# Pooled values of batch 0: four plain slices summed by GpSimd instead of a chain of accumulating transfers

## The chip, the cores and the metric

The kernel runs on one core of one Trainium2 chip. The metric is device time in microseconds (us). Three runs of the kernel before gave a median of 879.14 us (875.92 to 881.02).

## The reference, cut to what matters

Attention over 4 batches, 8 heads, 576 tokens and 64 dimensions per head is followed by two feed-forward layers over the 2304 tokens (512 wide inside 2048). The attention has two parts that are added: a local one over a window of 7 tokens, and a pooled one over averages of 4 tokens, whose result is repeated four times.

```python
q_d = q.reshape(B, H, Sd, factor, D).mean(axis=3)    # factor = 4, Sd = 144
k_d = k.reshape(B, H, Sd, factor, D).mean(axis=3)
v_d = v.reshape(B, H, Sd, factor, D).mean(axis=3)
out_d = sm_attn(q_d, k_d, v_d)
out_up = np.repeat(out_d, factor, axis=2)
...
return (out_up + out_local)
...
h = x @ w_in;  r = np.maximum(h, 0.0);  y = (r * r) @ w_out
...
h = y @ w_in2; out = (h * (1.0 / (1.0 + np.exp(-h)))) @ w_out2
```

The change is about `v_d` of batch 0 only: the sum of four slices of v, each 72 rows by 2 by 512 numbers (288 KB).

## The kernel before, in words

The kernel writes its whole program from generators that a planner (`Schedule`, line 90 on) interleaves. A generator yields the engine it wants next and a cost in us, or an event it waits for, or a lock on one of the PSUM banks; the planner starts whatever can start first by those costs, and ties go to the lower rank. The order in which it lets the generators go on is the order of instructions on each engine's queue; at run time every queue works strictly in that order, and semaphores only make it wait. So a changed cost or a changed event moves instructions of all later stages in the queues.

**The first stage.** Before the first feed-forward matmul the kernel does the attention of the first 512 tokens: `load_qk(0, h)` loads q and k of four head pairs by SyncE (SP), `load_pooled(0)` loads the pooled values, `load_v0` two halves of v, and `eighth("i1", 0)`, `eighth("o1", 0)` the first weights, which arrive as 64-bit numbers and are turned to float32 by ScalarE (line 312) and VectorE (helpers at 268 and 271). For each head pair `pooled(0, hp, SIX)` sums q and k (line 458 or 465), multiplies them (475), takes the softmax (479 to 492), transposes it (498 and 500) and multiplies it with the pooled values (510); ScalarE copies the product out (513). `tile_attention(i, SIX)` does the local attention of 64 tokens at a time, eight of them: scores (586, 589), softmax on VectorE and ScalarE (599 to 617), transposes (626), product with v (638). `tiles_done(0)` (890) adds the two, and gives the event ("xf", 0), on which the first feed-forward matmul (`chunk_in`, line 1027, then 1049) and the second batch's attention hang. All these share six PSUM banks, `pa`, `pb` and `acc0` to `acc3`, through locks. Gaps that the planner sees on TensorE in this stage are filled by `keep_warm` (1540).

**What the steps touch.** `load_pooled(0)` (line 405 on) issues four DMAs from GpSimd's queue (412): the first writes the tile `vd_t`, the three others add to it on the way, and each waits for the one before. `pooled` asks for the bank of its last product before it waits for the event ("pooled", 0). Behind these DMAs on GpSimd's queue stand those of batch 1 (422) and later the sums of batch 1 (432, 434). On SP's queue `load_qk(0)` is followed by one half of v (560), the first weights (304), the other half of v and the second weights. The tile `gr`, which the change uses as a buffer, holds the hidden values of the feed-forward layer from its first chunk on.

Of the kernel before, what the change touches and what calls it, by code (L numbers as in the profile page):

```python
# [13 lines left out]
ALU = mybir.AluOpType  # L14
# [4 lines left out]
NT, DM, DFF = 2304, 512, 2048  # L19
# [11 lines left out]
HG = NG // 2  # L31
# [63 lines left out]
class Schedule:  # L95
# [15 lines left out]
    def mark(self, key):  # L111
        self.events[key] = self.end

    def release(self, name):
        self.locks[name] = self.end
# [59 lines left out]
def tile_attention_two_moes(ctx: ExitStack, tc: tile.TileContext, qw, kw, vw, qt, kt, vt, qp, kp, vp, maskd, tmaskd,  # L175
                            w_in1, w_out1, w_in2, w_out2, out, wide):
    nc = tc.nc
# [5 lines left out]
    V, A, G, PE = nc.vector, nc.scalar, nc.gpsimd, nc.tensor  # L183
# [16 lines left out]
    gr = pool.tile([P, 7 * 512], F32, name="gr")  # L200
# [23 lines left out]
    def words(a, n):  # L224
        return wt[:, a:a + n]
# [40 lines left out]
    def ts(out, in0, s1, op0, s2=None, op1=None):  # L266
        kw_ = {"op1": op1} if op1 is not None else {}
        V.tensor_scalar(out=out, in0=in0, scalar1=s1, scalar2=s2, op0=op0, **kw_)
# [16 lines left out]
    def bank(name, shape):  # L285
        return ps1.tile(shape, F32, tag=name, name=name)
# [105 lines left out]
    def raw_buf(at, n=2048):  # L392
        return words(int(at), n).bitcast(U32)
# [4 lines left out]
    vd_t = dst[0:HG, 4 * NGP + 4 * NG:].rearrange("p (c n) -> p c n", c=2)  # L398
# [6 lines left out]
    def load_pooled(b):  # L405
        yield "DVE", 0.1
        V.memset(qd_t[:, :, NG:], 0.0)
        if b == 0:
            for r in range(4):
                yield "POOL", 1.1  # L410
                yield "DMA", 0.82, 2.0
                G.dma_start(out=vd_t, in_=vp[0, r], **({"accum_op": ALU.add} if r else {}))
        else:
            for r in range(4):
                kw_ = {"accum_op": ALU.add} if r else {}
                if b > 1:
                    yield "POOL", 2.1
                    G.dma_start(out=qd_t[:, :, :NG], in_=qp[b - 2, r], **kw_)
                    G.dma_start(out=kd_t, in_=kp[b - 2, r], **kw_)
                yield "POOL", 1.1  # L420
                yield "DMA", 1.5 if b == 1 else 4.5, 2.0
                G.dma_start(out=vd_t, in_=vp[b, r], **kw_)
        outd[b] = p2.tile([P, 4, NG], F32, tag="outd", name="outd")
        mark(("pooled", b))
# [12 lines left out]
    def pooled(b, hp, banks):  # L437
        pad = PADS[b]
        if b > 1:
            yield "event", ("pooled", b)  # L440
        elif b == 1:
            yield "event", ("sums", b, hp)
        if b == B - 1:
            w = words(hole["o2"] * 1024, 1024)
            yield "event", ("o2", "done")
        elif b == 0 and hp >= 2:
            w = hl[1][:, (hp - 2) * 1024:(hp - 1) * 1024]
        else:
            w = words(EX + (hp % 2) * 1024, 1024)
        n = 1 if b == B - 1 else 2  # L450
        if b:
            yield "event", ("ds", b, hp - n) if hp >= n else ("ds", b - 1, 3 if b > 1 else hp)
        if b == 0:
            yield "event", ("qk", 0, hp)
            for t, src, dve in ((qd_t[:, hp, :NG], qb[:, hp, :], hp in QDVE), (kd_t[:, hp, :], kb[:, hp, 3:3 + S], hp in KDVE)):
                if dve:
                    yield "DVE", 0.67, 0.0
                    V.tensor_reduce(out=t, in_=src.rearrange("p (g r) -> p g r", r=4), axis=AX.X, op=ALU.add)
                    continue
                ba = yield "lock", banks  # L460
                yield "PE", 1.0
                ps = bank(ba, [P, NG])
                src = src.rearrange("p (g r) -> p r g", r=4)
                for r in range(4):
                    PE.matmul(out=ps, lhsT=ident, rhs=src[:, r, :], start=(r == 0), stop=(r == 3))
                yield "ACT", 0.17
                A.activation(out=t, in_=ps, func=AF.Copy)
                release(ba)
        ba = yield "lock", banks
        yield "PE", 0.8, pad  # L470
        ps = bank(ba, [P, 3, NG])
        for c in range(3):
            for j in range(2):
                r = slice(j * D, (j + 1) * D)
                PE.matmul(out=ps[r, c, :], lhsT=qd_t[r, hp, c * QC:c * QC + D], rhs=kd_t[r, hp, :],
                          start=True, stop=True)
        yield "DVE", 0.71, pad
        mx = p2.tile([P, 3], F32, tag="dmx", name="dmx")
        V.tensor_reduce(out=mx, in_=ps, axis=AX.X, op=ALU.max)
        ts(mx, mx, -1.0 / 128.0, ALU.mult)  # L480
        yield "ACT", 1.07, pad
        e = w[:, 0:3 * NG].rearrange("p (c n) -> p c n", c=3)
        pt = w[0:HG, 3 * NG:7 * NG].rearrange("p (k j c q) -> p k j c q", k=2, j=2, c=3)
        sm = p2.tile([P, 3], F32, tag="dsm", name="dsm")
        for c in range(3):
            A.activation(out=e[:, c, :], in_=ps[:, c, :], func=AF.Exp, scale=1.0 / 128.0, bias=mx[:, c:c + 1],
                         accum_out=sm[:, c:c + 1])
        release(ba)
        yield "DVE", 0.93, pad
        ts(sm, sm, 1e-9, ALU.add, 4.0, ALU.mult)  # L490
        V.reciprocal(sm, sm)
        V.tensor_tensor(out=e, in0=e, in1=sm.unsqueeze(2).to_broadcast([P, 3, NG]), op=ALU.mult)
        for kc in range(2):
            ba = yield "lock", banks
            yield "PE", 0.33, pad
            pp = bank(ba, [HG, 3, 2, D])
            for c in range(3):
                PE.transpose(pp[:, c].rearrange("p j q -> p (j q)"), e[:, c, kc * HG:(kc + 1) * HG], ident)
            yield "ACT", 0.29, pad
            A.activation(out=pt[:, kc].rearrange("p j c q -> p c j q"), in_=pp[:, :, :, 0:QC], func=AF.Copy)  # L500
            release(ba)
        ba = yield "lock", banks
        if b < 2:
            yield "event", ("pooled", b)
        yield "PE", 0.6
        po = bank(ba, [P, NG])
        for kc in range(2):
            for j in range(2):
                h = 2 * hp + j
                PE.matmul(out=po[j * D:(j + 1) * D, :], lhsT=vd_t[:, kc, h * D:(h + 1) * D],  # L510
                          rhs=pt[:, kc, j].rearrange("p c q -> p (c q)"), start=(kc == 0), stop=(kc == 1))
        yield "ACT", 0.17
        A.activation(out=outd[b][:, hp, :], in_=po, func=AF.Copy)
        release(ba)
        mark(("ds", b, hp))
# [1031 lines left out]
    with tc.manual_schedule():  # L1547
# [40 lines left out]
        for h in range(4):  # L1588
            add(load_qk(0, h))
        add(load_pooled(0))  # L1590
        convert(0)
        for h in range(2):
            add(load_v0(h))
        for hp in range(4):
            add(pooled(0, hp, SIX))
# [4 lines left out]
        for n in range(1, 16):  # L1600
            convert(n, *([("qk", 0, 3)] if n == 1 else [("at", 3)] if n < 4 else []))
            if n == 3:
                add(split_early(0))
            if n == N1:
                add(load_pooled(1), ("xf", 0))
                for h in range(2):
                    add(load_qk(1, h), ("xf", 0))
                for hp in range(4):
                    add(sums(1, hp), ("xf", 0))
                for hp in range(4):  # L1610
                    add(pooled(1, hp, TWO))
                add(all_pooled(1))
                for i in range(per, 2 * per):
                    add(tile_attention(i, TWO), ("xf", 0))
                add(tiles_done(1))
            if n % 4 == 3 and n >= NFULL:
                add(quarter("i1", n // 4), ("xf", 0))
                add(quarter("o1", n // 4), ("xf", 0))
                add(first_scales(0, 1, n // 4))
# [4 lines left out]
        add(whole("o1"))  # L1624
        add(split_early(1))
        add(load_pooled(2), ("ds", 1), ("at", TPB - 1))
        for hp in range(4):
            add(pooled(2, hp, TWO))
# [14 lines left out]
        r = [[raw_buf(a * 1024)] for a in (22, 26, 28)]  # L1643
# [4 lines left out]
        r = [[gr[:, 1536 + i * 1024:2560 + i * 1024].bitcast(U32) for i in range(2)], [raw_buf(31 * 1024)]]  # L1648
# [122 lines left out]
```

## Time and profile before

| what | us |
|---|---|
| median of three runs | 879.14 |
| lowest and highest run | 875.92, 881.02 |
| span of the profiled execution | 882.3 |
| TensorE busy in it | 851.1 (96%) |
| VectorE busy in it | 673.6 (76%) |
| ScalarE busy in it | 524.6 (59%) |
| GpSimd busy in it | 59.7 (7%) |

The profiled execution is a run of its own; its span, from the first instruction to the last, is the only time that the profile gives for it, and no time around the span is shown. It is 3.2 us longer than the median and 1.3 us longer than the slowest of the three runs. The profile lists, for each engine, when it was busy and what released it after a wait; all times inside it count from the first instruction. TensorE's clock has two levels, 1.2 and 2.4 GHz, and the granted clock is given as a share of the higher one.

### The profile page before, as it was taken

The page shows a single profiled execution, that of the slowest core. Times are in us where ns is not written, and L with a number is a line of the kernel's source. Part 1 is how long each engine was busy: PE and PEld are TensorE (multiplying, and loading weights), DVE is VectorE, ACT ScalarE, POOL GpSimd, SP SyncE. Part 2 cuts the span into 40 slices and gives each one's busy share as a digit, 9 for nine tenths or more (in the row PEclk, how much of TensorE's full clock was granted, in tenths as well). Part 3 has the DMA queues.
Part 4 walks back from the last instruction along what each step waited for, and adds up shares of the span by engine and source line. Part 5 has one row for each costly group of instructions (what it writes and reads, how often), then busy time and mean ns, then how long its engine had stood idle before and what let it go on. Part 6 is the DMA issues. An engine that isn't in the chain of part 4 may idle for free.

```text
span 882.3 us, 14418 instructions
## 1 busy us (share of the span) xinstructions
PE 851.1 (96%) x5578; PEld 507.6 (58%) x5578; DVE 673.6 (76%) x1310; ACT 524.6 (59%) x1026; POOL 59.7 (7%) x86
## 2 busy tenths in 40 slices
PE   8898999999988999999999999999999899999998
PEld 6664554455433444444444445884445778788865
DVE  5567888886667999888988998746988887777731
ACT  3787888888767652435665443666676564344432
POOL 1016113000000400000000000000000110000000
PEclk9899999999999999999999999999999999999999
DMA  9678456844667951242124200322333200010010
GB/s 253 206 200 321 172 157 147 238 164 160 225 201 250 229 135 37 89 155 72 36 84 155 72 28 27 114 61 96 132 113 107 81 25 2 25 49 1 2 48 25
DMA packets 35584, 103.55 MB, mean 117 GB/s; under 512 B 4316, under 2 KB 8540, under 8 KB 32316
## 3 DMA queue, kind: packets, MB, share of 16 engines
q1 hardware_dynamic: 27036, 84.65, 29.0%
q0 software_dynamic: 8192, 17.83, 8.4%
q8 instruction: 44, 0.72, 0.3%
q14 instruction: 24, 0.20, 0.1%
q10 hardware_dynamic: 288, 0.15, 0.1%
HBM read 82.16 MB, written 20.45 MB: 116 GB/s over the span
## 4 chain that ended last, share of the span: by engine, by line
PE 71%; DMA 11%; DVE 8%; ACT 7%; issue 2%; POOL 1%; SPq 0%; POOLq 0%; DVEq 0%; ACTq 0%
PE acc L1106 26%; PE hps L1062 24%; PE seven L1181 6%; PE acc L1216 4%; DMA dst<-vp 4%; DMA wt<-w_in 3%; DMA gr<-w_out 3%; PE hps L1049 2%; DVE ub L1242 1%; DVE gr L271 1%; PE pb L1216 1%; DVE wt L271 1%; ACT sq L333 1%; PE hps L1027 1%; DVE hl L271 1%
## 5 line engine op out<-in xcount | busy, mean ns | idle before, releaser
L1062 PE MATMUL hps<-hl,wt 128*128 128x512 f16 (+1 forms) x1440 | 293.7, 351 | 0.0
L1062 PEld LDWEIGHTS <-wt 128*128 128x128 f16 x1440 | 140.2, 98 | 128.4 <-issue 3.6
L1106 PE MATMUL acc<-gr,wt 128*128 128x512 f16 (+2 forms) x928 | 212.8, 374 | 0.0
L1106 PEld LDWEIGHTS <-wt 128*128 128x128 f16 x864 | 84.5, 99 | 78.3 <-issue 1.2
L271 DVE SCALAR_TENSOR_TENSOR gr<-hps,sc,gr 128x512 f16<-128x512 f32 (+1 forms) x118 | 80.2, 679 | 63.2 <-ACT gr L1476 60.4
L1106 PE MATMUL acc<-wt,gr 128*128 128x512 f16 x480 | 112.0, 379 | 0.1
L1458 ACT ACTIVATE hps<-hps,sc 128x512 f32<-128x512 f32 (+1 forms) x72 | 44.0, 611 | 90.5 <-PE hps L1062 90.2
L1181 PE MATMUL seven<-hl,wt 128*128 128x256 f16 x456 | 80.5, 275 | 5.7 <-DVE ub L1242 5.6
L1473 ACT ACTIVATE hps<-hps,sc 128x512 f32<-128x512 f32 (+1 forms) x46 | 27.4, 596 | 91.5 <-PE hps L1062 87.6
L1106 PEld LDWEIGHTS <-gr 128*128 128x128 f16 x480 | 46.8, 98 | 51.8 <-issue 0.7
L1181 PEld LDWEIGHTS <-wt 128*128 128x128 f16 x672 | 66.1, 98 | 17.9 <-issue 7.5
L1476 ACT ACTIVATE gr<-hps,sc 128x512 f16<-128x512 f32 (+1 forms) x118 | 74.3, 630 | 2.7
L1216 PEld LDWEIGHTS <-gr 128*128 128x128 f16 x672 | 65.6, 98 | 11.0 <-DVE gr L271 2.0
L1216 PE MATMUL acc<-wt,gr 128*128 128x256 f16 x480 | 61.0, 274 | 2.2 <-DVE gr L271 1.1
L1181 PE MATMUL seven<-ub,wt 128*128 128x256 f16 x180 | 49.6, 275 | 0.0
L1242 DVE TENSOR_TENSOR ub<-seven,ub 128x256 f32<-128x256 f32 x74 | 28.6, 419 | 21.8 <-PE seven L1181 20.0
L271 DVE SCALAR_TENSOR_TENSOR wt<-wt,sc 128x1024 f16<-128x1024 f32 x32 | 40.6, 1279 | 4.7 <-ACT wt L372 4.4
L778 DVE TENSOR_REDUCE ub<-ub 128x128 f32<-128x896 f32 x40 | 43.3, 1083 | 1.0
L711 DVE TENSOR_TENSOR ub<-ub,s 128x896 f32<-128x896 f32 x40 | 43.5, 1087 | 0.6
L746 DVE TENSOR_REDUCE s<-ub 128x14 f32<-128x896 f32 x40 | 43.2, 1080 | 0.5
L708 DVE TENSOR_TENSOR ub<-ub 128x896 f32<-128x896 f32 x40 | 43.2, 1081 | 0.0
L271 DVE SCALAR_TENSOR_TENSOR gr<-ub,sc,gr 128x512 f16<-128x512 f32 (+2 forms) x66 | 42.1, 671 | 0.7 <-ACT gr L1476 0.7
(247 smaller groups left out, 1159.1 us busy)
## 6 DMA issues: line engine op xcount, KB each, us to landing
wt<-w_in SPq DMA_DIRECT2D x16, 1024.0 KB, 8.2
wt<-w_out SPq DMA_DIRECT2D x9, 1024.0 KB, 5.5
w<-wt POOLq DMA_DIRECT2D x16, 512.0 KB, 4.6
dst<-w SPq DMA_DIRECT2D x16, 512.0 KB, 3.3
gr<-w_out SPq DMA_DIRECT2D x14, 512.0 KB, 5.4
ub<-vw SPq DMA_DIRECT2D x10, 640.0 KB, 3.8
ub<-kw SPq DMA_DIRECT2D x10, 640.0 KB, 7.2
dst<-vp POOLq DMA_DIRECT2D x16, 288.0 KB, 6.9
```

The source lines that it names most:

```text
L271: V.scalar_tensor_tensor(out=out, in0=in0, scalar=s, in1=in1, op0=op0, op1=op1)
L708: eng.tensor_tensor(out=prod[i % 2].rearrange("p (t w d) -> p t w d", t=2, w=WIN), in0=band(k, j, t0), in1=q[:, j, t0:t0 + 2, :].unsqueeze ...
L711: eng.tensor_tensor(out=prod[i % 2].rearrange("p (t d w) -> p t d w", t=2, d=D), in0=band_v(v, j, t0), in1=prob[u][:, j, t0:t0 + 2, :].uns ...
L746: V.tensor_reduce(out=s[:, j, t0:t0 + 2, :], in_=prod[i % 2].rearrange("p (t w d) -> p t w d", t=2, w=WIN), axis=AX.X, op=ALU.add)
L778: V.tensor_reduce(out=o[:, t0:t0 + 2, j, :], in_=prod[i % 2].rearrange("p (t d w) -> p t d w", t=2, d=D), axis=AX.X, op=ALU.add)
L1062: PE.matmul(out=ps, lhsT=w[:, o:o + P], rhs=x[:, kk, :n], start=(m == 0), stop=(m == 3 * KD - 1))
L1106: PE.matmul(out=a, lhsT=l, rhs=x, start=(first and m == 0), stop=(last and m == len(ops) - 1))
L1181: PE.matmul(out=b7[:, i * 256:(i + 1) * 256], lhsT=a[:, c:c + P], rhs=x, start=(n == 0), stop=(n == 5))
L1216: PE.matmul(out=acc7[p][m][:, t, :], lhsT=a, rhs=b, start=(e == 0 and t == 0 and n == 0), stop=(e == 7 and t == 1 and n == 2))
L1242: V.tensor_tensor(out=out, in0=a, in1=b, op=op)
L1458: A.activation(out=ps, in_=ps, func=AF.Relu, scale=1.0 if exact else cs)
L1476: A.activation(out=gh, in_=ps, func=AF.Copy, scale=sg)
```

## The change

```diff
         if b == 0:
-            for r in range(4):
-                yield "POOL", 1.1
-                yield "DMA", 0.82, 2.0
-                G.dma_start(out=vd_t, in_=vp[0, r], **({"accum_op": ALU.add} if r else {}))
+            vr = gr[0:HG, 0:3 * 2 * DM].rearrange("p (r c n) -> p r c n", r=3, c=2)
+            yield "DMA", 4.0, 2.0
+            nc.sync.dma_start(out=vd_t, in_=vp[0, 0])
+            nc.sync.dma_start(out=vr, in_=vp[0, 1:4].rearrange("r p c n -> p r c n"))
+            for r in range(3):
+                yield "POOL", 2.1
+                G.tensor_tensor(out=vd_t, in0=vd_t, in1=vr[:, r], op=ALU.add)
...
-        ba = yield "lock", banks
         if b < 2:
             yield "event", ("pooled", b)
+        ba = yield "lock", banks
         yield "PE", 0.6
         po = bank(ba, [P, NG])
```

The first slice goes to `vd_t` and the other three to a buffer in `gr`, by two DMAs on SP's queue, right behind q and k. GpSimd then adds the three to `vd_t`, one after the other, each 72 partitions by 1024 float32 numbers. In `pooled` the event and the lock change places, for batches 0 and 1: a bank is asked for only once the pooled values are there.

## Rows read from the trace of the kernel before

**Rows 1.** The page, part 1: busy us, share of the span, instructions
```profile
PE 851.1 (96%) x5578; PEld 507.6 (58%) x5578; DVE 673.6 (76%) x1310; ACT 524.6 (59%) x1026; POOL 59.7 (7%) x86
```

**Rows 2.** The chain that ended last, 0 to 70 us: start, us, what
```profile
1.47 7.07 DMA dst<-vp
...
8.84 11.71 DMA dst<-vp
...
20.83 6.68 DMA dst<-vp
...
27.79 5.82 DMA dst<-vp
...
33.66 0.71 PE pb L510 x8
...
36.19 0.79 PE pb L498 x3
36.97 1.71 PE acc L626 x8
...
50.88 6.67 PE hps L1027 x30
```

**Rows 3.** Waits of all engines, 0 to 60 us: total, times, longest
```profile
POOL dst L412 <- DMA dst<-vp: 23.9, 3, 11.1
...
DVE asm L268 <- ACT ae L604: 7.9, 3, 6.4
...
PE pb L510 <- DMA dst<-vp: 1.8, 1, 1.8
...
ACT wt L312 <- DMA wt<-w_in: 1.6, 1, 1.6
```

**Rows 4.** Windows: length, busy us of each engine, granted clock, DMA share, GB/s
```profile
33.66:41.90 8.24, 8.24 (x88) 6.59 (x89) 1.23 (x5) 4.55 (x20) 0.00 (x0) 0.59 0.83 337
...
75.00:320.00 245.00, 236.20 (x1398) 116.43 (x1397) 194.39 (x403) 193.91 (x365) 45.45 (x63) 0.99 0.67 203
320.00:680.00 360.00, 358.71 (x1956) 187.97 (x1955) 300.56 (x506) 189.45 (x349) 0.00 (x0) 1.00 0.25 84
```

**Rows 5.** The chain that ended last, 50 to 175 us
```profile
94.43 0.33 PE pa L498 x3
...
96.70 0.64 PE pa L510 x8
...
101.19 0.44 PE pb L626 x4
```

**Rows 6.** Timeline, 24 to 36 us and 33 to 52 us: start, us
```profile
30.45 0.45 DVE L617 TENSOR_TENSOR ae<-ae,asm 128x280 f32<-128x280 f32 x1
...
36.77 1.91 PE L626 MATMUL acc<-ident,ae 128*70 128x128 f32 x8
```

**Rows 7.** Groups of GpSimd over the span: busy us, mean ns, idle before
```profile
L434 POOL TENSOR_TENSOR dst<-dst,ub 128x144 f32<-128x144 f32 x16 | 11.2, 701 | 1.3
...
L1400 POOL TENSOR_TENSOR dst<-xi,dst 128x256 f32<-128x256 f32 x4 | 3.0, 741 | 0.2
```

**Rows 8.** Timeline, 74.6 to 77 us, VectorE and GpSimd
```profile
74.39 0.75 DVE L271 SCALAR_TENSOR_TENSOR hl<-wt,sc,hl 128x512 f16<-128x512 f32 x1
74.66 1.54 POOL L434 TENSOR_TENSOR dst<-dst,ub 128x144 f32<-128x144 f32 x2
...
75.23 0.44 DVE L614 TENSOR_REDUCE asm<-ae 128x4 f32<-128x280 f32 x1
...
75.70 0.53 DVE L268 TENSOR_SCALAR asm<-asm 128x4 f32<-128x4 f32 x1
...
76.17 0.44 POOL L432 TENSOR_TENSOR dst<-ub 128x144 f32<-128x144 f32 x1
```

**Rows 9.** Groups of VectorE, 15.4 to 24.4 us: first and last of 15
```profile
L492 DVE TENSOR_TENSOR wt<-wt,dsm 128x432 f32<-128x432 f32 x2 | 1.2, 608 | 0.1
...
L268 DVE TENSOR_SCALAR amx<-amx 128x4 f32<-128x4 f32 x1 | 0.2, 169 | 0.0
```

**Rows 10.** DMA of the first 27 us: queue, packets, MB, share of 16 engines
```profile
q1 hardware_dynamic: 2028, 5.62, 73.1%
q0 software_dynamic: 287, 0.89, 14.9%
```

## The prediction

> **What bounds the kernel now.** I read the page first, then the chain that ended last, then the waits and windows of the stretch that the change touches. TensorE is busy for 96% of the span [rows 1], and from 75 us on it hardly stops: 236.20 of 245 us and 358.71 of 360 us [rows 4]. Time is therefore saved or lost where TensorE starts its long run late, that is ahead of the first feed-forward matmul. There the chain is the chain of accumulating transfers: four pieces of 7.07, 11.71, 6.68 and 5.82 us, 31.3 us in all, end in the product at line 510 at 33.66 us, and 17 us later the feed-forward matmuls run on the chain without a break, from 50.88 us [rows 2]. GpSimd itself waited 23.9 us between the four issues [rows 3]. Two things happen where the chain ends. TensorE waits 1.8 us for the last slice [rows 3]. And from there to 41.90 us it is busy all 8.24 us at a mean granted clock of 0.59, so most of that at the lower of its two levels, 1.2 GHz [rows 4]; before it fell TensorE had stood idle for those 1.8 us. The same work shows it: a group of three transposes takes 0.79 us [rows 2] and 0.33 us at full clock [rows 5]; eight at line 626 take 1.71 us [rows 2], four take 0.44 us at full clock [rows 5].
>
> **The change part by part.**
>
> *The transfers.* Four slices are 1.18 MB. In the first 27 us the plain queue moved 5.62 MB in 73.1% of the 16 engines' time, or 0.285 MB for each us of all of them; GpSimd's queue moved 0.89 MB in 14.9%, or 0.221 [rows 10]. The plain transfers need 1.18 / 0.285 = 4.1 us behind q and k (2.3 MB, 8.1 us from the start), so they end near 13 us; 2 us more is my estimate for the landing, and the adds start near 15 us (13 to 18). In front of v and the first weights on SP's queue these 4.1 us are new, but 0.149 x 27 = 4.0 us of accumulating packets leave the same engines. I take 0 for what stands behind them, SP's two more issues included. The bounds are 1.6 us less (ScalarE's wait for the first weights [rows 3] could go) and 2.0 us more (half of the 4.1 us). The buffer costs nothing: `gr` is first written by the feed-forward stage, after 50.88 us [rows 2].
>
> *The adds.* No add of 1024 elements is in the trace. The nearest rows are contiguous adds of 256 at 741 ns, and adds of 144 at stride four at 701 ns, both with waits in them [rows 7]. In proportion to the elements these give 3.0 and 5.0 us; with the slope between the two rows, 0.36 ns an element, it would be 1.0 us, which I keep as the lower end. I take 2.8 us, a little under the contiguous row because part of its 741 ns is per instruction: three adds, 8.4 us, ending near 24 us. Even at 5.0 us each they end by 33 us, before the 33.66 us of now. So the wait goes in every case: -1.8 us.
>
> The Trainium skill, "GPSIMD Engine Reference", section 3.1, gives 4497 ns for an add of 2048 float32 elements; from it I estimate 2.25 us for 1024, so 6.7 us for three, which would leave 1.7 us less in the term below. No run here shows it yet.
>
> *The slow clock.* 8.24 us at 0.59 would be 4.9 us at full clock: -3.4 us, if TensorE is not stalled so long elsewhere in this stage; 0 if it is.
>
> *The banks.* Tile 2's probabilities are ready at 30.45 + 0.45 = 30.90 us, and their transposes start at 36.77 us [rows 6]. Of these 5.9 us, 1.8 us are the wait, and in the 3.1 us after 33.66 us TensorE did three products and one group of transposes, 3 x 0.64 + 0.33 = 2.25 us at full clock [rows 5]. With the event ahead of the lock the planner no longer keeps three of the six banks for products that cannot start, and the transposes can go in front of them. I take -2.2 us, from 0 (the planner fills the place with other work) to -3.1 us.
>
> *What the adds take from VectorE.* This is the cost that the diff does not show. At 75.70 us VectorE starts a tensor_scalar on 4 columns while GpSimd is inside two adds (74.66 to 76.20 us); it takes 0.53 us and ends at 76.23 us, just behind the add [rows 8]. One of the same size takes 169 ns otherwise [rows 9]. The tensor_reduce at 75.23 us runs 0.44 us beside the same adds, not lengthened [rows 8]. The first of the two adds in turn does not end before the scalar_tensor_tensor that began at 74.39 us does: the pair takes 1.54 us, where the add behind them takes 0.44 [rows 8]. So some VectorE work and a GpSimd add exclude each other for a whole instruction. The adds fall into 15 to 24 us. VectorE's 15 groups from 15.4 to 24.4 us sum to 8.3 us, of which 5.0 us are tensor_tensor, scalar_tensor_tensor and tensor_scalar, and 3.3 us reduces, reciprocals and one operation that reads PSUM [rows 9]. If an excluded operation is always next, each add lets VectorE do only the free kind: 8.4 - 3.3 - 0.7 (what it was idle in these 9.0 us) = 4.4 us of delay. The bounds are 0 (VectorE waits 6.4 us for ScalarE later in this stage [rows 3], which could take it all up) and 3 x 5.0 - 4.0 = 11 us. I take 4.4 us, since the later idle time is itself a result of the stall that goes.
>
> The Trainium skill, "SBUF — State Buffer", section "Who interferes with whom", speaks against this change: GpSimd has no port pair of its own but VectorE's second one, and whichever starts first holds it for the whole instruction, while reduces stay out of it. The trace agrees in the 0.53 us against 0.169 us above; without such a rule the sum below would be 4.4 us lower, which is the first rival.
>
> *GpSimd's queue.* It loses four issues and the waits between them, and batch 1's transfers stand behind the adds now; they wait for the products at 510 anyway, which read the same tile. Cost 0; if the adds were the last to end, it would be their overhang, at most the 5 us of one add, on work of the second batch.
>
> **Sum.** -1.8 - 3.4 - 2.2 + 4.4 = -3.0 us at the end of the first stage. Since TensorE is busy nearly all the time after it [rows 4], I pass it on whole; 236.20 of 245 us bounds this below by 0.96. The profiled span of 882.3 us would become 879.3 us; against the median of 879.14 us, which lies 3.2 us under that span, it is **876.1 us**.
>
> **The rivals.**
>
> *The adds cost VectorE little.* The delay falls 10 us ahead of the place where the chain now ends, and VectorE is busy for only 76% of the span [rows 1]. Then only -7.4 us remains, or -6.4 us with 1 us left of the exclusion: 871.7 to 872.7 us. Against it speaks that VectorE is busy 8.3 of 9.0 us just there [rows 9].
>
> *The adds stop the softmax, slower.* The place is 15 to 30 us. If an add takes the 5.0 us of the strided row, VectorE falls 11 us behind; TensorE, which waits for its probabilities, stands idle for more than the 1.8 us after which its clock fell before, and pays 3.4 us at the lower level again. That is -7.4 + 11 = +3.6, or +7.0 us with the slow stretch: 882.7 to 886.1 us, in the middle 884.4. It decides from the point where VectorE loses more than 7.4 us on the path. For it speaks how exactly the 0.53 us ends with the add; against it that the new adds are contiguous, as the 741 ns row is.
>
> *The gain is lost behind the first stage, or the change moves nothing there.* The planner may fill the place of the transposes with other work (-2.2 us gone), and later stages are planned anew: weights that are loaded at a time of their own would then be late for an earlier TensorE. TensorE's idle 8.8 us from 75 to 320 us [rows 4] say that there are such places. Then it is 879.1 us, some 3 us either way.
>
> **How the numbers follow.** A measurement of this kernel can tell about 0.5%, 4.4 us, from no change: faster means under 874.7 us, slower over 883.5 us. The forecast gets 0.48, with a range of its own of 873 to 879 us, of which 0.14 lies under 874.7 us. The first rival gets 0.26, all faster. The second gets 0.16, of which 0.13 is slower. The third gets 0.10: 0.08 within, 0.02 slower. Faster is 0.14 + 0.26 = 0.40, within 0.5% 0.34 + 0.03 + 0.08 = 0.45, slower 0.15. The range reaches down past the first rival's 871.7 us by the 1.6 us of ScalarE's wait, to 870.5 us with a little left out, and up to 883.5 us, into the second rival; about 0.1 lies beyond each end.
>
> **What would show it.** Right: no wait of line 510 for a transfer; line 510 before 30 us; the three adds between 13 and 30 us at 2.2 to 3.2 us each; VectorE operations of 1 to 3 us among them where 0.2 to 0.6 us is usual; line 1027 starting about 3 us earlier, and as much at the end of the span. Wrong: adds of 5 us; a stretch with the lower clock in the first 50 us; line 1027 earlier but the end not; VectorE operations beside the adds at their usual length.

## The result, and the profile after

The changed kernel takes 890.27 us (median of 4 runs, 888.38 to 893.60), the kernel before 878.88 us (4 runs, 875.92 to 881.02) on the same chip: ratio 1.0127, 95% interval 1.0082 to 1.0171. It is slower by 11.4 us; the forecast was 876.1 us, and the range ended at 883.5 us. The two profiles show less, 886.6 against 882.3 us of span: the profile of after is of its fastest run (888.38 us, so 1.8 us lie around the span), that of before, whose span would come to some 884 us with as much around it, is of a run slower than any of its four. Ratios and intervals below leave out one run of e2 and one of e5 that lay over 1.5% above the fastest of their kernel, and a ratio need not be the quotient of the medians beside it.

The page of the changed kernel, part 1 (busy us, share of the span, instructions), answers to [rows 1]:

```profile
PE 850.3 (96%) x5563; PEld 506.0 (57%) x5563; DVE 680.0 (77%) x1310; ACT 526.8 (59%) x1028; POOL 66.1 (7%) x85
```

The line numbers of the changed kernel are 3 higher behind the edit: 510 is now 513, 626 is 629, 1027 is 1030, 1062 is 1065.

**The first stage.** The timeline of the changed kernel, 16 to 34 us (start, us, engine and line, what; in brackets the idle time before it and what ended it), in three pieces: GpSimd, VectorE, TensorE.

```profile
18.92 7.28 POOL L415 TENSOR_TENSOR dst<-dst,gr 72x1024 f32<-72x1024 f32 x3 [17.61 <-DMA gr<-vp]
...
18.90 0.17 DVE L268 TENSOR_SCALAR dmx<-dmx 128x3 f32<-128x3 f32 x1
18.98 2.33 DVE L268 TENSOR_SCALAR asm<-asm 128x4 f32<-128x4 f32 x1
...
21.55 2.44 DVE L620 TENSOR_TENSOR ae<-ae,asm 128x280 f32<-128x280 f32 x1
23.92 0.43 DVE L617 TENSOR_REDUCE asm<-ae 128x4 f32<-128x280 f32 x1
24.38 1.84 DVE L268 TENSOR_SCALAR asm<-asm 128x4 f32<-128x4 f32 x1
...
24.05 0.63 PE L629 MATMUL acc<-ident,ae 128*70 128x128 f32 x4 [2.64 <-DVE ae L620]
27.07 1.04 PE L629 MATMUL pa<-ident,ae 128*70 128x128 f32 x4 [2.38 <-DVE ae L620]
```

The three adds take 7.28 us from the first start to the last end, 2.34 to 2.43 us each. One VectorE operation is held beside each: a tensor_scalar on 4 columns for 2.33 and 1.84 us instead of 0.17, a tensor_tensor on 280 columns for 2.44 instead of 0.45. That is 2.16 + 1.99 + 1.67 = 5.8 us. The reduce at 23.92 us is not lengthened. TensorE waits twice for what VectorE then delivers, 2.64 and 2.38 us. The long accumulating waits of GpSimd [rows 3] have become one wait of 17.61 us for the plain transfer, and the wait of line 510 is gone.

The windows of the changed kernel around this stretch (length, then busy us and instructions of PE, PEld, DVE, ACT, POOL, granted clock, DMA share, GB/s):

```profile
20.00:33.66 13.66, 8.64 (x113) 6.69 (x110) 11.57 (x19) 6.17 (x26) 6.04 (x3) 0.75 0.52 153
33.66:41.90 8.24, 8.02 (x135) 6.10 (x133) 6.96 (x22) 7.91 (x35) 0.00 (x0) 1.00 0.16 31
```

The second row covers the stretch that stood at 0.59 before [rows 4]: it is now at full clock. The first row is new: 5 us of the 13.66 TensorE is idle, and the mean clock is 0.75. In shorter windows of the same trace it is still 1.00 up to 25 us, behind the first of the two waits, and 0.50 to 0.53, so the lower level, from 25 us, within the second wait, to 32 us.

**The rest of the span.** TensorE by stage, in the changed kernel (same columns):

```profile
0.00:75.00 75.00, 64.19 (x623) 45.60 (x624) 53.62 (x117) 48.61 (x142) 11.07 (x13) 0.95 0.79 242
75.00:320.00 245.00, 236.78 (x1404) 117.52 (x1404) 193.00 (x397) 192.12 (x362) 49.41 (x64) 0.99 0.65 197
320.00:580.00 260.00, 257.14 (x1400) 133.16 (x1398) 225.02 (x347) 127.84 (x234) 0.00 (x0) 1.00 0.22 78
580.00:640.00 60.00, 57.17 (x319) 31.49 (x318) 37.58 (x88) 36.60 (x73) 0.00 (x0) 0.97 0.31 106
```

From 75 to 320 us TensorE is as busy as before. From 320 to 580 us it is idle 2.9 us, and from 580 to 640 us 2.8 us, where before it was idle 1.3 us in all the 360 us from 320 us on [rows 4]; and the clock falls in the last of these rows (0.97). The timeline of the changed kernel shows the place:

```profile
589.46 1.47 PE L1109 MATMUL acc<-gr,wt 128*128 128x256 f16 x12
593.36 0.38 PE L1065 MATMUL hps<-hl,wt 128*128 128x512 f16 x1 [2.42 <-ACT hl L878]
594.14 3.95 PE L1065 MATMUL hps<-hl,wt 128*128 128x512 f16 x11 [0.41 <-DVE hl L271]
...
599.51 2.75 PE L1065 MATMUL hps<-hl,wt 128*128 128x512 f16 x12
```

Eleven products take 3.95 us at 594.14 us; 5 us later, at full clock, twelve take 2.75 us. They wait for the input of the next feed-forward chunk, whose last unit of local attention VectorE finishes late: its last sum (line 532) starts at 581.3 us, and at 571.3 us in e10 below, a run with the order of the kernel before.

### The profile page after: what moved, and what is told of

Same layout as the page of the kernel before. It is cut to its first block, busy times and chain, and to the rows that moved or that the text cites. A ratio compares the mean times of both kernels' runs of the same rounds, so it can differ in the third digit from the quotient of the medians.

```text
span 886.6 us, 14388 instructions
## 1 busy us (share of the span) xinstructions
PE 850.3 (96%) x5563; PEld 506.0 (57%) x5563; DVE 680.0 (77%) x1310; ACT 526.8 (59%) x1028; POOL 66.1 (7%) x85
## 4 chain that ended last, share of the span: by engine, by line
PE 66%; DVE 19%; ACT 8%; DMA 4%; issue 2%; POOL 0%; SPq 0%; POOLq 0%; ACTq 0%; DVEq 0%
PE acc L1109 23%; PE hps L1065 23%; PE seven L1184 6%; PE acc L1219 4%; DVE gr L271 3%; DVE wt L271 2%; DVE ub L711 2%; DVE ub L1245 1%; DMA gr<-w_out 1%; DVE s L749 1%; DVE ub L781 1%; DVE ub L714 1%; DMA wt<-w_out 1%; DVE hl L271 1%; PE pb L1219 1%
## 5 line engine op out<-in xcount | busy, mean ns | idle before, releaser
L1065 PE MATMUL hps<-hl,wt 128*128 128x512 f16 (+1 forms) x1440 | 297.3, 353 | 2.8 <-ACT hl L878 2.4
L1109 PE MATMUL acc<-gr,wt 128*128 128x512 f16 (+2 forms) x928 | 210.4, 373 | 0.0
```

What stands on the lines that cost most here:

```text
L1065: PE.matmul(out=ps, lhsT=w[:, o:o + P], rhs=x[:, kk, :n], start=(m == 0), stop=(m == 3 * KD - 1))
L1109: PE.matmul(out=a, lhsT=l, rhs=x, start=(first and m == 0), stop=(last and m == len(ops) - 1))
```

## The experiments

Three theories stood at the start. **P**: the adds hold VectorE up, as seen above. **O**: the new order costs; a changed cost and a changed event move instructions of all later stages in the queues. **T**: the plain transfers push back what stands behind them on SP's queue. "Old order" below is the order of the kernel before.

### The change's instructions in the old order

**e1**: the costs that the planner sees and the order of event and lock stay as in the kernel before; only the instructions are changed.

```diff
+            vr = gr[0:HG, 0:3 * 2 * DM].rearrange("p (r c n) -> p r c n", r=3, c=2)
             for r in range(4):
                 yield "POOL", 1.1
                 yield "DMA", 0.82, 2.0
-                G.dma_start(out=vd_t, in_=vp[0, r], **({"accum_op": ALU.add} if r else {}))
+                if r == 0:
+                    nc.sync.dma_start(out=vd_t, in_=vp[0, 0])
+                    nc.sync.dma_start(out=vr, in_=vp[0, 1:4].rearrange("r p c n -> p r c n"))
+                else:
+                    G.tensor_tensor(out=vd_t, in0=vd_t, in1=vr[:, r - 1], op=ALU.add)
```

> The plan of the kernel before, cost for cost, so every engine keeps its old order; only the four accumulating transfers are replaced by the two plain ones and three GpSimd adds, issued at the old places. If the adds holding VectorE up is what counts (theory P), the 5.2 us that the wait and the slow clock cost are given back as 5 to 6 us of VectorE delay: 877 to 881 us, VectorE operations of about 2 us beside the adds. If the new order of the instructions is what counts (theory O), the old order with the early values gains: 872 to 875 us. If neither, the time goes to that of the changed kernel, 888 us or more.

Measured: 884.88 us (12 runs) against 879.92 (29 runs), ratio 1.0049 (1.0028 to 1.0071). The time lies between those named for P and for neither theory, and above O's. So 5 us come without any new order.

**e5**: as e1, without the `else` branch.

> The kernel before with its old order and the two plain transfers, and the three adds left out (pooled values of batch 0 from the first slice alone): against the run with the old order and the adds it differs by the adds alone, against the kernel before by the transfers alone. Theory T (the plain transfers push the first weights back, which land at 26.6 instead of 20.9 us): the loss of 4.4 us stays nearly whole, 883 to 886 us. Theory P (the adds hold VectorE up): it is back at the kernel before or better, 874 to 880 us.

Measured: 887.34 us (7 runs) against 878.90 (13), ratio 1.0067 (1.0031 to 1.0104). Without the adds it is no faster (it lies even above T's range by its median), so in this order the adds are not what costs. The waits from 12 to 45 us name what does (engine, line, what was waited for: us, times, longest); e1 first, then e5:

```profile
ACT wt L312 <- DMA wt<-w_in: 7.5, 1, 7.5
...
PE acc L503 <- ACT wt L505: 6.6, 1, 6.6
```

```profile
ACT wt L312 <- DMA wt<-w_in: 7.4, 1, 7.4
...
PE acc L501 <- ACT wt L503: 6.5, 1, 6.5
```

ScalarE waits 7.5 us for the first weights where it waited 1.6 us before [rows 3]. Behind its conversion (line 312) on ScalarE's queue stands the copy of transposed probabilities (line 500 of the kernel before), and TensorE waits for that: 6.6 us. That is T.

**e7**: the two plain transfers are issued one step later (`if r == 1`), behind the first weights on SP's queue, and the adds stand behind the loop. **e8**: as e7, with the adds on VectorE (`V.tensor_tensor`). **e13**: as e7, one step later still (`if r == 2`), behind both halves of v and both first weights.

> The old order, plain transfers and three GpSimd adds, but the two transfers stand behind the first weights in SP's queue. Theory T: the first weights land near 21 us again, and the loss of the run with the transfers in front goes: 876 to 881 us. Theory P: the adds still hold VectorE up for 4 to 6 us, only later, and the time stays at 882 to 886 us.

> As the run before in this call, with the three adds on VectorE at the same place of the order. They cost VectorE about 3 x 1.2 = 3.6 us of its own instead of up to 5.8 us of waiting. Theory P: 1 to 3 us less than with GpSimd's adds. If the exclusion costs nothing on the path, VectorE's own 3.6 us make it 0 to 3 us more.

> The order of the kernel before, with the plain transfers issued behind v and the first weights of both kinds on SP's queue, and the three adds on GpSimd behind the loop. T (what costs in the old order is that the plain transfers push back whatever stands behind them): v and the first weights land as in the kernel before, TensorE does not wait 5 to 7 us near 22 us, and the time is 879 to 882 us. P (the adds cost): the adds now fall beside the last softmaxes of the stage and hold them up, 883 to 886 us.

Measured: e7 883.74 us (7 runs) against 878.90 (13), ratio 1.0058 (1.0035 to 1.0082); e8 888.01 us (6 runs) against the same, 1.0102 (1.0070 to 1.0133); e13 887.08 us (6 runs) against 879.98 (11), 1.0084 (1.0057 to 1.0112). Waits from 12 to 45 us, e7, then e13:

```profile
DVE dmx L484 <- PE acc L480: 6.9, 1, 6.9
...
PE acc L643 <- DMA wt<-vt: 5.1, 1, 5.1
```

```profile
POOL dst L417 <- DMA gr<-vp: 27.4, 1, 27.4
...
PE pb L515 <- POOL dst L417: 6.4, 1, 6.4
```

In e7 the weights are in time, and the second half of v is late instead: TensorE waits 5.1 us for it, and again stands idle, from 23 to 28 us. The time is in P's range, but the wait is not P's. In e13 TensorE waits for neither weights nor v, but the slices themselves are late: they are there at 28.7 us, the adds follow, and the product waits 6.4 us for them. And P shows once more; the timeline of e13 beside the adds:

```profile
28.68 7.60 POOL L417 TENSOR_TENSOR dst<-dst,gr 72x1024 f32<-72x1024 f32 x3 [27.37 <-DMA gr<-vp]
...
28.92 2.31 DVE L268 TENSOR_SCALAR dsm<-dsm 128x3 f32<-128x3 f32 x1
...
31.48 2.61 DVE L497 TENSOR_TENSOR hl<-hl,dsm 128x432 f32<-128x432 f32 x1
34.01 2.30 DVE L268 TENSOR_SCALAR asm<-asm 128x4 f32<-128x4 f32 x1
```

In e8 the three adds take VectorE 1.22 us each, half of GpSimd's time, and the time is 4.3 us above e7's by the medians: v is late again (6.8 us), and the product waits another 1.7 us for the adds, which VectorE reaches in its own order only at 36.3 us.

So T's expectation for e13 missed: wherever the 1.18 MB stand on SP's queue, something is late for them, weights, v or the slices, and TensorE waits 5 to 7 us once. All three places cost 0.5 to 0.8%.

### The order

**e9** changes only what the planner is told that the accumulating transfers cost. The work stays; the plan also sets which bank a step takes and how many fillers `keep_warm` puts in (47 for 50):

```diff
             for r in range(4):
                 yield "POOL", 1.1
-                yield "DMA", 0.82, 2.0
+                yield "DMA", 0.9, 2.0
```

> The kernel before with one number of the planner changed: a slice of the pooled values is planned at 0.9 instead of 0.82 us of DMA time. No instruction is added, removed or altered, only the order. Theory O (any new order of the later stages costs, since the priorities were set for the old one): 884 to 889 us. Otherwise 878 to 881 us, as before.

Measured: 891.28 us (6 runs, 888.31 to 897.78) against 878.90 (13), ratio 1.0152 (1.0119 to 1.0185). A new plan of the same work costs as much as the whole change.

**e6** gives the kernel before exactly the change's order, with the accumulating chain kept: the change's yields and its exchange of event and lock, but `G.dma_start(..., accum_op=ALU.add)` in the place of each add and `G.dma_start` for the first slice; in its trace and in the change's, TensorE, VectorE and ScalarE do the same operations in the same order. **e10** was meant to have 0.7 in place of 0.82, and so its expectation reads. The kernel that ran has 0.83:

```diff
-                yield "DMA", 0.82, 2.0
+                yield "DMA", 0.83, 2.0
```

With 0.83 the planner gives the old order: in e10's trace all 5578 matmuls, every operation of VectorE, ScalarE and GpSimd and every transfer of SP's queue follow one another as in the trace of the kernel before. So e10 is the kernel before, run again.

> The change's order of all instructions, but the four slices brought by the accumulating chain on GpSimd's queue as before: no adds, no plain transfers. P (the adds hold VectorE up) and T (plain transfers push the first weights back): both of their causes are gone, so it is back near the kernel before, 878 to 882 us. O (the order costs): the order is the change's, so the units' VectorE work is late again, TensorE stands idle for 2 to 3 us near 590 us, and the time is 886 to 892 us.

> The kernel before with the planner's cost for the accumulating transfers 0.7 in place of 0.82: again only the order changes, but here the planner keeps the units' work of 320 to 580 us at its places. O in its form 'the units' VectorE work becomes late and TensorE waits near 590 us': no stall there, 878 to 882 us. O in its form 'the priorities fit one order, and any other order costs': slower by 0.5% or more, 883 us and up. P and T: nothing they speak of is changed, 879 us.

Measured: e6 895.47 us (6 runs) against 880.27 (20), ratio 1.0181 (1.0152 to 1.0209); e10 880.95 us (12 runs) against the same, 1.0012 (0.9991 to 1.0032). In the change's order the chain is the worse of the two by the medians, 895.47 against 890.27 us; TensorE waits for it again, in the waits of e6 from 12 to 45 us:

```profile
PE acc L512 <- DMA dst<-vp: 4.9, 1, 4.9
```

e10 tests neither form of O; its 1.0012 shows how closely two sets of runs of one order agree, and that a changed cost need not move anything.

| instructions | old order | 0.9 (e9) | the change's order |
|---|---|---|---|
| accumulating chain | 1, and 1.0012 (e10) | 1.0152 | 1.0181 (e6) |
| plain transfers and adds | 1.0049 (e1) | | 1.0127 |

The shares do not add up: the new instructions cost 5 us in the old order, and in the change's order they are no dearer than the chain. The broad form of O, that any other order costs, is not refuted: all seven other orders that ran (the change's, and those of e3, e4, e9, e11, e12 and e14) are slower than the old one, by 0.6 to 1.8%, four of them tried with the chain (e4, e6, e9, e14). That this is because the priority table was set for the old order is O's reason, and not shown.

Where the order's share is lost shows in the windows of e10, a run of the old order, and e9, stage by stage (columns as above), e10 first:

```profile
0.00:75.00 75.00, 67.68 (x664) 47.23 (x664) 50.24 (x127) 52.69 (x150) 11.61 (x21) 1.00 0.84 255
75.00:320.00 245.00, 236.85 (x1389) 116.39 (x1390) 193.59 (x397) 190.98 (x359) 41.30 (x58) 0.99 0.66 197
320.00:580.00 260.00, 258.70 (x1432) 136.40 (x1431) 225.38 (x352) 125.34 (x235) 0.00 (x0) 1.00 0.23 75
580.00:640.00 60.00, 60.00 (x321) 31.12 (x319) 41.13 (x89) 40.43 (x77) 0.00 (x0) 1.00 0.33 110
```

```profile
0.00:75.00 75.00, 66.93 (x638) 46.22 (x639) 47.15 (x117) 50.58 (x147) 7.71 (x15) 1.00 0.80 241
75.00:320.00 245.00, 235.13 (x1398) 115.57 (x1397) 191.44 (x394) 190.74 (x358) 46.09 (x64) 0.99 0.65 197
320.00:580.00 260.00, 257.15 (x1396) 132.90 (x1395) 225.67 (x349) 127.10 (x233) 0.00 (x0) 1.00 0.23 79
580.00:640.00 60.00, 57.13 (x324) 31.75 (x323) 37.13 (x87) 36.77 (x74) 0.00 (x0) 0.97 0.32 105
```

The spans are 876.4 and 886.5 us. Length less busy time gives TensorE's idle time. In e9 it is 0.75, 1.7, 1.55 and 2.9 us more than in e10, stage by stage, and 0.3 us more behind 640 us: 7.2 of the 10.1 us. The other 2.9 us are longer busy time, which I can't split up. In the changed kernel, by its windows above, the same sum against e10 is 3.5, 0.1, 1.6 and 2.8 us, less 0.8 us at the end: 7.2 of its 10.2 us, and 3.0 us of longer busy time. From 320 to 640 us, then, the two kernels lose the same, and the wait near 590 us is the same one, 2.5 us in e9:

```profile
PE hps L1062 <- ACT hl L875: 2.5, 1, 2.5
```

One more reading splits a span in two: the start of line 1049's first product (1052 in the changed kernel). In every order the same 512 matmuls stand ahead of it, besides `keep_warm`'s fillers. One profile of each kernel, some from a short run of it and some from a long one, so 2 us between two kernels say little:

| order | profiles | first product of line 1049, us | rest of the span, us |
|---|---|---|---|
| old, with the chain | before, b1, b2, e10 | 57.40, 57.94, 53.20, 52.64 | 824.9, 823.5, 826.2, 823.8 |
| old, plain transfers | e1, e5, e7, e8, e13 | 60.43, 59.80, 57.87, 61.14, 59.76 | 826.6, 827.0, 824.3, 822.6, 823.8 |
| the change's | the change, e6 | 57.68, 59.71 | 828.9, 829.8 |
| e9's, e14's, e3's | e9, e14, e3 | 55.04, 61.64, 53.93 | 831.5, 832.5, 835.1 |
| e4's, e11's, e12's | e4, e11, e12 | 58.34, 59.86, 55.42 | 824.0, 825.8, 825.0 |

In the old order the rest is the same, 822.6 to 827.0 us, whether the first stage ends at 52.6 or at 61.1 us. In five of the eight profiles of other orders it is longer.

**e11** takes the priorities of three units (`('unit', 8): 52`, `('unit', 9): -135`, `('unit', 10): -57`) out of the changed kernel's table. **e14** does the same to e9. **e12** sets twelve entries of the changed kernel's table anew for its own order: those three out, a new one for unit 13, seven others moved (such as `('tile_attention', 11)` from 32 to 7) and one taken out.

> The changed kernel with the three priorities of units 8, 9 and 10 taken out of the table, so that the units are planned anew; the first stage, the plain transfers and the adds stay as they are. O (units late): the stall of 2.4 us near 590 us and the slow stretch behind it go, some 4 us: 884 to 887 us, and DVE's last unit is at most 2 us later than in the kernel before. P and T: the first stage is untouched, so the time stays at 889 to 891 us.

> The changed kernel with eleven entries of the priority table set anew for its own order (the three unit priorities out, one in for unit 13, seven others moved, one out). O: with an order that is fitted to the change, the lead that the first stage wins is kept: 878 to 883 us, about the kernel before or a little under it. P and T: what the adds take from VectorE and the late first weights stay, so not under 884 us, the time of the change's instructions in the old order.

> The kernel before with the planner's cost at 0.9, as in the run that was as slow as the change, and with the three priorities of units 8, 9 and 10 taken out of the table. O (those priorities fit the old order alone, and the units' late VectorE work is what costs): no wait of TensorE near 590 us, 883 to 887 us. If something else in the order costs, the wait goes or stays and the time stays at 889 to 893 us.

Measured: e11 887.08 us (6 runs) against 880.27 (20), ratio 1.0087 (1.0059 to 1.0115); e12 886.22 us (9 runs) against the same, 1.0064 (1.0037 to 1.0091); e14 892.55 us (6 runs) against 879.98 (11), 1.0133 (1.0104 to 1.0162). The wait near 590 us shrinks from 2.42 to 0.62 us in e11, and the eleven products behind it take 2.54 us, so at full clock:

```profile
594.07 0.38 PE L1062 MATMUL hps<-hl,wt 128*128 128x512 f16 x1 [0.62 <-ACT hl L875]
594.86 2.54 PE L1062 MATMUL hps<-hl,wt 128*128 128x512 f16 x11 [0.41 <-DVE hl L268]
```

In e14 it shrinks to 0.6 us as well, and yet e14 is as slow as e9. So the late units near 590 us are a place where time is lost, worth some 3 us by the medians of e11 and the change (the intervals overlap) and nothing in e9's order, but not the cause of the order's whole cost. A table set for the change's own order (e12) gives about half of the loss back by the ratios, whose intervals overlap a little. What it is in e9's order that costs the rest was not settled.

### The parts within the change

**e2** is the changed kernel without its three adds, **e3** the changed kernel with event and lock as before, **e4** the kernel before with the exchange alone:

```diff
-        ba = yield "lock", banks
         if b < 2:
             yield "event", ("pooled", b)
+        ba = yield "lock", banks
```

> The changed kernel with the three adds left out: the pooled values of batch 0 are the first slice alone, and order, transfers and buffer stay. Theory P: VectorE loses no 5.8 us beside the adds, and the time falls by 4 to 8 us, to 882 to 886 us. Theory O: the order is unchanged, so the time stays within 2 us of the changed kernel, 888 to 892 us.

> The changed kernel with event and lock in the old order: a bank is asked for before the pooled values are there. If the exchange of event and lock is what made the order bad (theory O, by the exchange), it is 880 us or less. If the order is bad by the new transfer costs, or theory P holds, it stays at 886 to 892 us.

> The kernel before with the exchange of event and lock alone; the four accumulating transfers stay. My prediction's step on the banks says 2.2 us less than before, 876 to 877 us. Theory O, by the exchange, says slower: 884 to 890 us. Theory P alone says no change, 877 to 881 us.

Measured, against 879.92 us: e2 888.35 us (12 runs), ratio 1.0079 (1.0051 to 1.0107); e3 889.45 us (6 runs), 1.0089 (1.0060 to 1.0119); e4 885.21 us (12 runs), 1.0071 (1.0042 to 1.0101). The exchange gains nothing in either kernel, and alone it costs 5.3 us. Leaving the adds out saves 1.9 us by the medians and 0.5% by the ratios, whose intervals overlap. That is not the price of the adds alone, for without them another wait shows: the first weights stand behind the same plain transfers, and in e2's profile (of its longest run) TensorE waits for what they hold up, as in e1. Its waits from 12 to 45 us:

```profile
ACT wt L312 <- DMA wt<-w_in: 4.3, 1, 4.3
...
PE acc L500 <- ACT wt L502: 3.5, 1, 3.5
```

In the change itself no engine waits for the first weights.

### The kernel before, profiled again

> The kernel before, profiled once more. If the lower clock behind the wait of line 510 belongs to every run of it, the first stage has again a stretch of about 7 us at the lower level, the first feed-forward matmul is at 49 to 50 us, and the time is near 884 us. If only some runs have it (theory D: the profile that the prediction rested on was a late run), there is none, the first feed-forward matmul is 4 to 5 us earlier, and the time is 876 to 881 us.

> The same once more: with a slow stretch behind the wait of line 510 near 884 us, without it 876 to 881 us.

Measured: 883.40 and 881.54 us. The windows over the 8.2 us behind the wait of line 510, in b1, b2 and e10 (the kernel before by its order), answer to the first of [rows 4]:

```profile
34.20:42.40 8.20, 8.16 (x86) 6.74 (x87) 0.87 (x5) 4.35 (x18) 0.00 (x0) 0.60 0.85 332
```

```profile
32.30:40.50 8.20, 7.99 (x136) 6.75 (x136) 3.40 (x13) 6.89 (x28) 0.55 (x1) 1.00 0.95 360
```

```profile
31.80:40.00 8.20, 7.98 (x136) 6.77 (x136) 3.16 (x13) 6.85 (x28) 0.54 (x1) 1.00 0.96 354
```

Line 510 waits 1.9 us in b1, and the clock falls to 0.60; it waits 1.1 and 1.4 us in b2 and e10, and the clock stays at full level. The times are 883.40, 881.54 and 878.47 us. So the slow stretch is in some runs of the old order and not in others, two of four profiles, and the prediction's was one that had it. Line 1049 starts at 57.40 and 57.94 us with it and at 53.20 and 52.64 us without (table above).

## Why the prediction was wrong, step by step

**Passing the gain on whole** is the step that failed most. It was right that TensorE is busy nearly all the time behind the first stage, and in the old order a first stage that ends earlier or later is indeed passed on whole. It was wrong that the change stays in that order: with its own, what follows line 1049's first product takes 828.9 us, against 823.5 to 826.2 us in four profiles of the old one with the chain, and a new plan of the old instructions costs 12 us (e9) or 15 us (e6) in all. Nor was there a gain to pass on: see the sum below. The third rival named this ("later stages are planned anew") and sized it at some 3 us either way; it is four to five times that, and the result lies beyond the range for it. Late input for an earlier TensorE was its mechanism, and the wait near 590 us is of that kind, though on VectorE's units and not on weights.

**The slow clock, -3.4 us.** The stretch behind line 510 is gone as forecast, but it moved to 20 to 33.66 us, behind the two new waits (0.75 in the windows above). And it should not have been taken from the median: b2 and e10, at 881.54 and 878.47 us, have no such stretch and nothing of it to give back, and the median lies between them. The gain was read from a run 3 us above the median and taken off the median.

**The transfers, 0 us, from -1.6 to +2.0.** ScalarE's first conversion, in the timeline of the kernel before and then of the changed one:

```profile
20.91 1.13 ACT L312 ACTIVATE wt<-wt 128x1024 f32<-128x1024 f32 x1 [1.56 <-DMA wt<-w_in]
```

```profile
28.63 1.11 ACT L312 ACTIVATE wt<-wt 128x1024 f32<-128x1024 f32 x1
```

It starts 7.7 us later, but here it waits for no transfer; ahead of it on ScalarE's queue stand copies (line 632) that wait for TensorE. The price of the transfers shows by itself in e1, in the old order:

```profile
26.62 1.12 ACT L312 ACTIVATE wt<-wt 128x1024 f32<-128x1024 f32 x1 [7.51 <-DMA wt<-w_in]
```

There the conversion starts 5.7 us later than before, and waits for its weights. The DMA engines' free share was the wrong measure: the accumulating chain took its 4.0 us in pieces spread over 27 us, while the plain transfers take theirs at once, in front of the first weights. In the old order this is the whole price, 0.5% (e1) to 0.7% (e5), some 4 to 6 us; in the change no wait for it shows.

**What the adds take from VectorE, +4.4 us.** Right in kind and size: 5.8 us, within the bounds, and the reduce between the held operations ran free. In the Trainium skill, "SBUF — State Buffer", section "Who interferes with whom", GpSimd uses VectorE's second port pair, and whichever is first holds it for the whole instruction. Here the holds of 2.33 and 2.44 us beside adds of 2.34 to 2.43 us agree. What it costs at the end, 2 to 4 us by e2, is not told from nothing.

**The adds, 2.8 us each, ready near 24 us.** Measured 2.34 to 2.43 us each, and ready at 26.2 us: they started at 18.92 us instead of 15, since the transfers landed later. The estimate from the Trainium skill, "GPSIMD Engine Reference", section 3.1, 2.25 us, is the nearer one.

**The wait, -1.8 us**, went, as forecast, but line 510's products started at 33.23 us (line 513), not before 30: the two waits for VectorE stand ahead of them. **The banks, -2.2 us**: not won; e3 against the change shows no gain by the exchange, and e4 a loss; it too changes the order. **GpSimd's queue, 0**: nothing was seen that speaks against it.

**The sum at the end of the first stage, -3.0 us.** The first half of line 1027's products starts at 45.43 us in the changed kernel (line 1030), at 49.56 us in the prediction's profile and at 44.81 us in e10; the second half waits for VectorE. The changed kernel's timeline, then e10's:

```profile
45.43 0.60 PE L1030 MATMUL hps<-wt 128*128 128x256 f32 x2
...
54.12 3.72 PE L1030 MATMUL hps<-wt 128*128 128x256 f32 x16 [1.42 <-DVE wt L893]
57.68 2.84 PE L1052 MATMUL hps<-wt 128*128 128x512 f32 x6
```

```profile
44.81 0.70 PE L1027 MATMUL hps<-wt 128*128 128x256 f32 x2
46.06 6.74 PE L1027 MATMUL hps<-wt 128*128 128x256 f32 x30
52.64 3.70 PE L1049 MATMUL hps<-wt 128*128 128x512 f32 x8
```

Against e10, a run of the old order without the slow stretch, the first stage ends 5.0 us later (57.68 against 52.64), not 3.0 us earlier; against the prediction's own profile, where line 1049 starts at 57.40 us, it ends level, 0.3 us later. Of the second rival, that the adds stop the softmax, the mechanism came true: two stalls, each longer than the 1.8 us, and a new slow stretch. Its price was for adds of 5.0 us that cost VectorE 11 us, and these took half of that; of the change's 10.2 us against e10, 5.2 us were lost behind this stage. How much of the 5.0 us in it is the adds' and how much the order's was not settled: e9's order alone ends it 2.4 us later than e10.

## What to carry to other kernels

Where a planner lays out all queues, an edit to a cost, an event or a lock can be an edit to the whole program (0.9 for 0.82 was, 0.83 was not): compare the orders of instructions in the traces first, then measure the edit's order with the old instructions, and the new instructions in the old order, before reading anything into the sum. Take gains from the run that the profile shows only against that run: a stall that some runs have and others don't is not in the median. And ask of a transfer not how much engine time it takes but what stands behind it on its queue at that moment.

## What the runs showed of the hardware that was not expected

Runs of one order can differ by a whole slow stretch: with line 510's wait at 1.8 and 1.9 us (the prediction's profile and b1) the next 8.2 us ran at 0.59 and 0.60 of the clock, with 1.1 and 1.4 us (b2 and e10) at 1.00. What sets the wait's length from run to run was not tried, nor whether it is the wait's length that decides.

Adds of 1024 float32 columns on GpSimd took 2.34 to 2.43 us each (7.28 us for three) in the changed kernel and 2.34 to 2.58 us (7.60 us) in e13, against 1.22 us on VectorE (e8), and in both each one held one VectorE operation, in e13 for 2.31, 2.61 and 2.30 us; tensor_scalar and tensor_tensor alike, down to operations on 3 columns.
